# Rewriting a gather-heavy kernel: one product per batch of gathers, four key sets per search, and an order planned by the kernel itself

## The chip, the cores and the metric

The kernel runs on one core of one Trainium2 chip. The metric is device time in microseconds (us), lower is better. The names of the engines are those of the profile: PE multiplies matrices (PEld loads its weights), DVE is the vector engine, ACT the engine for activations, POOL the general one that also issues the gathers, SP the one that issues most other transfers.

## The reference

`x` is A_q, 2048 tokens of 448 numbers; `xn` is its layer norm. The output is x + A(xn) + B(xn).

```python
def A(q, k, v, shift_k, ssm_k, ssm_D):
    kv = causal_conv4(k, shift_k) * v                    # per channel, 4 taps
    y = irfft(rfft(kv, 4096) * rfft(ssm_k, 4096))[:2048]  # per channel, along the tokens
    return q * (y + kv * ssm_D)

def B(x, w_q, k1, k2, u, v):                 # 16 heads, 64 keys of 256 numbers in k1 and in k2
    q = einsum("nd,dhc->nhc", x, w_q)        # c = 512: one half for k1, one for k2
    s1, s2 = q[..., :256] @ k1.T, q[..., 256:] @ k2.T      # (2048, 16, 64) each
    # the two best of s1 and of s2 make four sums; the two best sums are two experts
    # out of 64 * 64, with softmax weights g
    act = gelu(einsum("nd,nhkd->nhk", x, u[top_e]))
    return einsum("nhk,nhk,nhkd->nd", g, act, v[top_e])
```

Each token so needs 32 rows of `u` and 32 of `v`, by computed indices: 65536 rows of 896 numbers (u and v side by side), 235 MB.

## The kernel before

The 2048 tokens are 16 tiles T of 128. For each head, `weights` multiplies w_q by the keys, so that the scores are one product of the tokens with a 448 x 2048 matrix, held in two parts (high and low) for precision. `scores(T)` transposes a tile, makes 4 groups of 512 scores in PSUM (11 matmuls each, L198 to L202), and finds in each of the 32 sets of 64 keys the 8 largest (`max`, L205) and their places (`max_index`, L206); a dozen small DVE operations choose two experts per head, and DVE transposes write the indices to `idx`.

The experts' part works in batches: a batch is 4 gathers (`gather`, L253, an indirect DMA on POOL's queue), each of 128 rows of u and v, that is 4 tokens x 32 slots. There are 8 batches k per tile, 128 in all, and a ring of 12 buffers of one gather. In `dots`, a matmul with `sel` (L266) copies each of the four token rows to its 32 partitions in PSUM, and DVE multiplies with the gathered rows and sums (L268). `values` applies gelu and gate (ACT L271, DVE L276) and multiplies with the v half of the rows into one PSUM bank `pv` (L279). `fold` adds a finished tile to `acc`.

The convolution is an FFT as matmuls: `conv_in` (taps, first stage, L335 to L362), `spectrum` (L372 to L383), `inverse` (L391 to L403), `conv_out` (L413 to L431), in two groups of 56 x 4 channels. It is cut into units with rough costs and follows the scores in one stream `work`; after every batch `fill` takes as many units as fit in the room of one batch:

```python
ROOM = (3.6, 2.9, 4.6, 0.7)
            with tc.high_priority(offset=500):
                dots(T, k)
                values(T, k)
                for o in order[4 * b + NBUF:4 * b + 4 + NBUF]:
                    gather(*o)
            fill(ROOM)
```

A scheduler of the framework orders the instructions of each engine from these priorities. PSUM has four pools of two banks.

Of the kernel before, what the change touches and what calls it, by code (L numbers as in the profile page):

```python
# [17 lines left out]
P = 128  # L18
S, D, H, E = 2048, 448, 16, 64
NT = S // P  # L20
KC = 3
KR = D - P * KC
# [9 lines left out]
GC = 56  # L32
BC = 8
KV0, H0, SK0, D0, BW = 67, 131, 195, 199, 200


def fft_tables():
# [32 lines left out]
    const = np.concatenate([f1.reshape(P, -1), ci.reshape(P, -1), tw.reshape(P, -1), f3.reshape(P, -1) / N], axis=1)  # L70
    return const.astype(np.float32), fq.reshape(NQ, P, P).astype(np.float32)


F1W, CIW, TWW, F3W = 2 * NQ * CH, 4 * P, 17 * 3, 16 * CH


@with_exitstack
def parallel_kernel(ctx, tc, x, wq, kk, uv, kvh, const, fq, out):
    nc = tc.nc
    ap = ctx.enter_context(tc.tile_pool(name="ap", bufs=1))  # L80
    rp = ctx.enter_context(tc.tile_pool(name="rp", bufs=2))
    gp = ctx.enter_context(tc.tile_pool(name="gp", bufs=NBUF))
    ps_sc = ctx.enter_context(tc.tile_pool(name="ps_sc", bufs=2, space=bass.MemoryType.PSUM))
    ps_xr = ctx.enter_context(tc.tile_pool(name="ps_xr", bufs=2, space=bass.MemoryType.PSUM))
    ps_a = ctx.enter_context(tc.tile_pool(name="ps_a", bufs=2, space=bass.MemoryType.PSUM))
    ps_v = ctx.enter_context(tc.tile_pool(name="ps_v", bufs=2, space=bass.MemoryType.PSUM))

    acc = ap.tile([P, NT, D], F32, name="acc")
    xn = ap.tile([P, NT, D], F32, name="xn")
    kks = ap.tile([P, 4, E], F32, name="kks")  # L90
    nc.scalar.dma_start(kks, kk)

    def load_x(t0, t1):
        nc.sync.dma_start(acc[:, t0:t1, :], x[t0:t1].rearrange("t p d -> p t d"))


    ident = ap.tile([P, P], F32, name="ident")
    sel = ap.tile([P, 64, 32], F32R, name="sel")
    rmask = ap.tile([P, 4], F32, name="rmask")
    cc = [ap.tile([P, 4, 32], F32, name=f"cc{k}") for k in range(8)]  # L100

    def sel_and_masks():
        make_identity(nc, ident)
        # sel[p, j, s] = 1 where p mod 64 == j
        nc.vector.tensor_add(sel, ident[:, 0:64, None].broadcast_to([P, 64, 32]),
                             ident[:, 64:128, None].broadcast_to([P, 64, 32]))
        # rmask[p, r] = 1 where p div 32 == r
        nc.vector.reduce_sum(rmask, ident.rearrange("p (r s) -> p r s", s=32), axis=mybir.AxisListType.X)
        for k in range(8):
            nc.gpsimd.memset(cc[k], 0.0)  # L110
# [6 lines left out]
    def norm(t0, t1):  # L117
        sl, n = slice(t0, t1), t1 - t0
        for t in range(t0, t1):
            st = rp.tile([P, 6], F32, tag="st", name="st")  # L120
            nc.vector.bn_stats(st, acc[:, t, :])
            nc.vector.bn_aggr(mv[:, t, :], st)
        # 1/sqrt(var + eps): a guess from the exponent, then Newton's steps to full precision
        va, y0, y1 = (rp.tile([P, NT], F32, tag=f"n{i}", name=f"n{i}")[:, :n] for i in range(3))
        nc.vector.tensor_scalar(va, mv[:, sl, 1], 1e-5, None, op0=ALU.add)
        nc.vector.tensor_scalar(y1.bitcast(I32), va.bitcast(I32), 1, None, op0=ALU.logical_shift_right)
        nc.vector.tensor_scalar(y0.bitcast(I32), y1.bitcast(I32), -1.0, float(0x5F3759DF), op0=ALU.mult, op1=ALU.add)
        for i in range(4):
            nc.vector.tensor_mul(y1, y0, y0)
            nc.vector.tensor_mul(y1, y1, va)  # L130
            nc.vector.tensor_scalar(y1, y1, -0.5, 1.5, op0=ALU.mult, op1=ALU.add)
            nc.vector.tensor_mul(y0 if i < 3 else rstd[:, sl], y1, y0)
        nc.vector.scalar_tensor_tensor(nmr[:, sl], mv[:, sl, 0], -1.0, rstd[:, sl], op0=ALU.mult, op1=ALU.mult)
        for t in range(t0, t1):
            nc.scalar.activation(xn[:, t, :], acc[:, t, :], AF.Identity, bias=nmr[:, t:t + 1], scale=rstd[:, t:t + 1])

    ws_ctx = ExitStack()
    wp = ws_ctx.enter_context(tc.tile_pool(name="wp", bufs=1))
    wh = wp.tile([P, KC, S], F32R, name="wh")
    wl = wp.tile([P, KC, S], F32R, name="wl")  # L140
    # the last 64 rows: high part above, low part below
    wr = wp.tile([P, S], F32R, name="wr")

    state = {}

    def transposes(pt, src, permute):
        for c in range(KC + 1):
            n = P if c < KC else KR
            o = pt[:n, P * c:P * c + P]
            if permute:  # L150
                o = o.rearrange("p (r c k) -> p c k r", r=4, c=4)
            nc.tensor.transpose(o, src[:, P * c:P * c + n], ident)

    def weights(h):
        ww = []
        for half in range(2):
            w = gp.tile([P, 2 * D], F32, tag="uv", name="wq")
            state["wq"] = nc.sync.dma_start(w.rearrange("p (c d) -> p c d", c=2),
                                                       wq[h, 2 * half:2 * half + 2].rearrange("c p d -> p c d"))
            ww.append(w)  # L160
        pw = ps_a.tile([P, 512], F32, tag="a", name="pw")
        for i in range(2):
            for half in range(2):
                nc.tensor.matmul(pw[64 * half:64 * half + 64, :D], kks[:, 2 * half + i, :], ww[half][:, D * i:D * i + D],  # L164
                                 start=(i == 0), stop=(i == 1), tile_position=(0, 64 * half))
        ws = wp.tile([P, D], F32, tag="ws", bufs=2, name="ws")
        nc.scalar.activation(ws, pw[:, :D], AF.Copy)
        pt = ps_xr.tile([P, 512], F32, tag="xr", name="pt")
        transposes(pt, ws, False)
        hs = slice(128 * h, 128 * h + 128)  # L170
        ptv = pt[:, :P * KC].rearrange("p (c n) -> p c n", c=KC)
        nc.scalar.activation(wh[:, :, hs], ptv, AF.Copy)
        nc.scalar.activation(wr[:KR, hs], pt[:KR, P * KC:], AF.Copy)
        nc.vector.tensor_sub(wl[:, :, hs], ptv, wh[:, :, hs].bitcast(F32))
        nc.vector.tensor_sub(wr[KR:, hs], pt[:KR, P * KC:], wr[:KR, hs].bitcast(F32))

    idx = ap.tile([P, NT, NG], I32, name="idx")
    gt = ap.tile([P, NT, NG], F32, name="gt")

    def scores(T):  # L180
# [353 lines left out]
```

## Time and profile before

| | |
|---|---|
| median of 3 runs | 1082.19 us (1070.23 to 1082.56) |
| profiled execution | span 1089.4 us |
| PE, DVE, ACT, POOL busy | 846.0, 771.3, 326.2, 551.0 us |
| bytes moved | 274.29 MB, mean 252 GB/s |
| mean granted PE clock | 0.860 |

The profile is of one execution, 7 us longer than the median; its own time is its span. A group of instructions is written as line, engine, operation, output <- input, count, then busy time and mean duration, then the idle time of the engine ahead of it and what ended most of it. In a timeline a row has start, duration, engine, line and operation. Durations on one engine can overlap by about a tenth of a microsecond, so the pitch from start to start is what counts in a full engine. Windows list the busy time of PE, PEld, DVE, ACT and POOL, and end with the granted PE clock, the DMA engines' busy share and GB/s.

### The profile page before, as it was taken

How to read it: one execution, taken by the hardware profiler on the slowest of the kernel's cores; microseconds unless marked ns; L12 is line 12 of the kernel's file. 1: busy time of each engine (PE TensorE's matmuls, PEld its weight loads, DVE VectorE, ACT ScalarE, POOL GpSimd, SP SyncE). 2: the span in 40 equal slices, each digit the busy share in tenths (PEclk: the TensorE clock that was granted, in tenths of full speed). 3: DMA queues.
4: the chain of work that ended last, by engine and by line, in shares of the span. 5: the costliest groups of instructions: out<-in, count | busy, mean ns of one | idle time of the engine just before them, and what ended most of it. 6: DMA issues, size and time to landing. Idle time of an engine off the chain costs nothing.

```text
span 1089.4 us, 15169 instructions
## 1 busy us (share of the span) xinstructions
PE 846.0 (78%) x4124; PEld 465.0 (43%) x4124; DVE 771.3 (71%) x3474; ACT 326.2 (30%) x952; POOL 551.0 (51%) x596
## 2 busy tenths in 40 slices
PE   7946778878968787777767667898987876789883
PEld 3422444434434444444433434354564443345472
DVE  4466667877789877787875545699947665599941
ACT  4313201111111110111114553366422564355421
POOL 1025255465656455455564354655558554555533
PEclk9975888888889888788986877899987888899987
DMA  9928458678778777577888776988767876888753
GB/s 340 338 95 296 152 202 270 201 273 270 267 238 263 253 252 249 200 252 259 270 274 313 257 264 204 305 284 285 254 236 268 285 256 233 292 276 268 243 200 135
DMA packets 65973, 274.29 MB, mean 252 GB/s; under 512 B 10336, under 2 KB 31200, under 8 KB 65888
## 3 DMA queue, kind: packets, MB, share of 16 engines
q0 software_dynamic: 40960, 234.91, 63.8%
q1 hardware_dynamic: 24784, 38.28, 10.1%
q8 instruction: 33, 0.54, 0.2%
q14 instruction: 52, 0.43, 0.1%
q10 hardware_dynamic: 144, 0.13, 0.0%
HBM read 269.61 MB, written 3.67 MB: 251 GB/s over the span
## 4 chain that ended last, share of the span: by engine, by line
PE 42%; DVE 32%; issue 12%; another core or an unknown queue 6%; ACT 3%; DMA 3%; POOL 1%; DVEq 0%; SPq 0%; POOLq 0%; ACTq 0%
DVE xr L268 11%; PE xr L266 8%; PE pv L279 7%; DVE mi L206 6%; PE ps L359 5%; DVE mx L205 4%; PE sc L198 3%; PE pw L164 3%; PE sc L199 3%; PE sc L200 3%; PE fin L420 3%; DVE tt L380 2%; DVE y L382 2%; ACT pr L339 2%
## 5 line engine op out<-in xcount | busy, mean ns | idle before, releaser
L253 POOL DMA_INDIRECT uv<-in_uv_dram,idx x512 | 492.2, 961 | 486.3 <-PE pv L279 139.0
L268 DVE SCALAR_TENSOR_TENSOR xr<-xr,uv 128x448 f32<-128x448 f32 x512 | 316.3, 625 | 114.0 <-remote 40.9
L266 PE MATMUL xr<-ab,sel 128*128 128x448 f32 x512 | 246.9, 518 | 144.1 <-DVE xr L268 97.2
L266 PEld LDWEIGHTS xr<-ab,sel 128*128 128x128 f32 x512 | 99.3, 210 | 293.9 <-DVE xr L268 173.4
L205 DVE MAX8 mx<-sc 128x8 f32<-128x64 f32 x512 | 110.3, 216 | 68.0 <-remote 30.0
L279 PE MATMUL pv<-uv,cc 128*32 128x448 f32 x1024 | 146.3, 648 | 8.7 <-DVE cc L276 6.6
L271 ACT ACTIVATE ge<-act 128x4 f32<-128x4 f32 x128 | 26.1, 204 | 325.6 <-DVE xr L268 210.3
L206 DVE FIND_INDEX8 mi<-mx,sc 128x8 uint32<-128x64 f32 x512 | 113.3, 222 | 0.1
L198 PE MATMUL sc<-wh,xh 128*128 128x512 f32 x192 | 89.9, 468 | 12.4 <-DVE xl L190 5.3
L199 PE MATMUL sc<-wl,xh 128*128 128x512 f32 x192 | 83.7, 436 | 0.1
L200 PE MATMUL sc<-wh,xl 128*128 128x512 f32 x192 | 82.5, 430 | 0.0
L268 DVE DVE_READ_ACCUMULATOR xr<-xr,uv 128x1 f32 x512 | 69.9, 136 | 0.6
L372 PE MATMUL psf<-x,fm 128*128 128x448 f32 x132 | 64.1, 573 | 2.1 <-issue 1.7
L362 ACT ACTIVATE x<-ps 128x396 f32<-128x396 f32 (+1 forms) x84 | 37.9, 458 | 83.8 <-PE ps L359 40.3
L198 PEld LDWEIGHTS sc<-wh,xh 128*128 128x128 f32 x192 | 42.2, 220 | 45.8 <-issue 26.8
L339 ACT ACTIVATE pr<-stg 128x64 f32<-128x64 f32 x224 | 56.0, 336 | 8.0 <-DMA stg<-in_kvh_dram 6.9
L359 PE MATMUL ps<-cst,stg 128*64 128x132 f32 x448 | 42.9, 339 | 16.1 <-DVE stg L349 9.2
L359 PE MATMUL ps<-cst,pr 128*64 128x132 f32 x448 | 40.0, 323 | 19.1 <-ACT x L362 8.4
L206 DVE MATCH_VALUE_LOAD mi<-mx,sc 128x8 f32 x512 | 42.7, 83 | 10.1 <-remote 1.7
L359 PEld LDWEIGHTS ps<-cst,stg 128*64 128x64 f32 x448 | 32.9, 170 | 35.0 <-issue 21.5
L199 PEld LDWEIGHTS sc<-wl,xh 128*128 128x128 f32 x192 | 42.3, 220 | 9.2 <-issue 0.7
L392 PE MATMUL psu<-y,cst 128*128 128x224 f32 x132 | 39.3, 380 | 8.9 <-DVE y L383 7.3
(98 smaller groups left out, 1069.3 us busy)
## 6 DMA issues: line engine op xcount, KB each, us to landing
wq<-in_wq_dram SPq DMA_DIRECT2D x32, 448.0 KB
stg<-in_kvh_dram SPq DMA_DIRECT2D x14, 800.0 KB
uv<-in_uv_dram,idx POOLq DMA_INDIRECT x512
fm<-in_fq_dram SPq DMA_DIRECT2D x66, 64.0 KB
out_dram<-acc SPq DMA_DIRECT2D x16, 224.0 KB
acc<-in_x_dram SPq DMA_DIRECT2D x2, 1344.0 KB
acc<-in_x_dram SPq DMA_DIRECT2D x1, 672.0 KB
cst<-in_const_dram SPq DMA_DIRECT2D x1, 445.5 KB
```

The costliest lines, as they stand in the source:

```text
L198: nc.tensor.matmul(sc, xh[:, c, :], wh[:, c, ns], start=(c == 0), stop=False)
L199: nc.tensor.matmul(sc, xh[:, c, :], wl[:, c, ns], start=False, stop=False)
L200: nc.tensor.matmul(sc, xl[:, c, :], wh[:, c, ns], start=False, stop=False)
L205: nc.vector.max(mx[:, 8 * n + j, :], sc[:, 64 * j:64 * j + 64])
L206: nc.vector.max_index(mi[:, 8 * n + j, :], mx[:, 8 * n + j, :], sc[:, 64 * j:64 * j + 64])
L253: nc.gpsimd.indirect_dma_start(buf, None, uv, bass.IndirectOffsetOnAxis(ap=idx[:, T, g:g + 1], axis=0))
L266: nc.tensor.matmul(xr[:, :D], sel[:, t:t + 4, :].rearrange("p a b -> p (a b)"), ab[c // 2], start=True, stop=True)
L268: nc.vector.scalar_tensor_tensor(xr[:, :D], xr[:, :D], 1.0, rows[T, k, c][:, :D], op0=ALU.mult, op1=ALU.mult, accum_out=act[:, c:c + 1])
L279: nc.tensor.matmul(pv[32 * c:32 * c + 32, :D], cc[k][:, c, :], rows.pop((T, k, c))[:, D:], start=(k == 0), stop=(k == 7), tile_position=(0 ...
L339: nc.scalar.activation(pr[t][:, c, :], stg[:, c, 3 - t:67 - t], AF.Copy, scale=stg[:, c, SK0 + t:SK0 + t + 1])
L359: nc.tensor.matmul(ps[64 * i:64 * i + 64, w * j:w * j + w], src, f1[:, i, :], start=True, stop=True, tile_position=(0, 64 * i))
L372: nc.tensor.matmul(ps[:, :2 * CH * GC], fm, x1[:, :, q, :, :].rearrange("p c t k -> p c (t k)"), start=True, stop=True)
```

## The change

The kernel is written anew around the same mathematics. By part:

- **Batches.** A gather now brings 32 tokens x 4 slots, so partition p of gather r belongs to token 32 r + p mod 32. `spread(T)` writes each quarter of a tile to all 128 partitions of one of four PSUM banks (`xs`) with a 32-row matmul, once per tile and not once per gather. One DVE multiplication of 4 x 448 takes a whole batch; ACT sums each of the four products; gelu on ACT; two POOL multiplications make the coefficients; four matmuls with blocks of 32 columns add up in one bank. The ring has 5 batches (20 buffers). A gather waits for the landing of the sixth before it.
- **Searches.** The two largest of 8 key sets stand side by side, and one `max_index` looks up the 8 values of four sets in their 256 scores. An index outside its own set is noted (`lo`, `hi`). After the pass a flag is loaded, and if it is set, a whole second pass (`safe`) runs with a search for every set.
- **Indices.** They come out of masks (ACT) and a matmul (`place`) instead of DVE transposes, for the first tile a quarter of the heads at a time.
- **Convolution.** Two parts, 28 and 84 of the 112 groups of 4 channels; the first runs beside the scores, the second after them. The four taps are one DVE multiplication; the tap additions are on POOL in the first part and on DVE in the second.
- **Output.** `fold` reloads `x`, adds `pv` and stores the tile. The convolution's part of tiles 0 to 13 is added in DRAM by 14 accumulating transfers, which stand at the end of POOL's queue; tiles 14 and 15 add it before their store.
- **Order.** A list planner (`Plan`) in the kernel sorts all operations by due times and assumed durations while the program is built; the framework keeps that order on each engine. PSUM holds `xs` (4 banks), `pv` (1) and 3 banks that all else shares.

The core of the diff:

```diff
-NG = 32
-NBUF = 12
-ROOM = (3.6, 2.9, 4.6, 0.7)
+NB = 8
+RING = 5
+PARTS = ((0, 28), (28, 84))
+T_OUT0, T_OUT1 = 9, 14
...
+class Plan:
+    def op(self, eng, dur, fn, r=(), w=(), key=0.0, acq=None, rel=None, nb=0.0, name="", after=()):
...
+T0, PACE, PACE2 = 51.5, 5.4, 4.5
+TURN = 58
+OUTSTANDING = 6
+LIGHT = 200
...
+    xs = pp.tile([P, 4, 512], F32, name="xs")
+    pv = pp.tile([P, 512], F32, name="pv")
+    bank = [pp.tile([P, 512], F32, name=f"bank{i}") for i in range(3)]
...
-            for j in range(8):
-                nc.vector.max(mx[:, 8 * n + j, :], sc[:, 64 * j:64 * j + 64])
-                nc.vector.max_index(mi[:, 8 * n + j, :], mx[:, 8 * n + j, :], sc[:, 64 * j:64 * j + 64])
+            for j in range(8):
+                nc.vector.max(mx[:, 8 * n + j, :] if safe else m2[:, n, 2 * j:2 * j + 8], bank[s.i][:, 64 * j:64 * j + 64])
+        def find(g):
+            if safe:
...
+            else:
+                nc.vector.max_index(m4i[:, 2 * n + g, :], m2[:, n, 8 * g:8 * g + 8], bank[s.i][:, 256 * g:256 * g + 256])
...
+                nc.vector.tensor_sub(loc[:, gs_], m4i[:, gs_], off8[:, None, :].broadcast_to([P, 2 * (b1 - b0), 8]))
+                nc.vector.tensor_tensor(lo[:, gs_], lo[:, gs_], loc[:, gs_], op=ALU.min)
+                nc.vector.tensor_max(hi[:, gs_], hi[:, gs_], loc[:, gs_])
...
-        nc.vector.transpose(idx[:, T, :], es.rearrange("p h t -> p (h t)"))
+            for q in range(4):
+                src = Ev.rearrange("p r k (j s) -> p s r k j", s=4)[:, q]
+                nc.tensor.matmul(o[32 * q:32 * q + 32, :8 * nj], rep, src, start=True, stop=True, tile_position=(0, 32 * q))
...
-            nc.tensor.matmul(xr[:, :D], sel[:, t:t + 4, :].rearrange("p a b -> p (a b)"), ab[c // 2],
-                             start=True, stop=True)
-            nc.vector.scalar_tensor_tensor(xr[:, :D], xr[:, :D], 1.0, rows[T, k, c][:, :D], op0=ALU.mult, op1=ALU.mult,
-                                           accum_out=act[:, c:c + 1])
+    def spread(T):
+            for r in range(4):
+                rs = slice(32 * r, 32 * r + 32)
+                nc.tensor.matmul(xs[:, r, :D], i4[rs, :], XA[rs, T, :], start=True, stop=True, tile_position=(32 * r, 0))
+    def batch(T, j):
...
+        op("DVE", dve(m * D), lambda: nc.vector.tensor_mul(U[:, :m, :], U[:, :m, :], xs[:, :m, :D]), r=["xs"], w=u[:m], key=k, name="prod")
...
+        for r in range(m):
+            op("ACT", 0.72, lambda r=r: nc.scalar.activation(U[:, r, :], U[:, r, :], AF.Copy, accum_out=aw[:, r:r + 1]),
...
+        def coef():
+            ve.tensor_mul(co, ge, gat[:, T % 8, :, j])
+            ve.tensor_mul(cc[b % 3], co[:, :, None].broadcast_to([P, 4, 32]), rep[:, None, :].broadcast_to([P, 4, 32]))
+        def val():
+            for r in range(4):
+                nc.tensor.matmul(pv[32 * r:32 * r + 32, :D], cc[b % 3][:, r, :], ring[:, b % RING, r, D:],
+                                 start=(j == 0), stop=(j == NB - 1), tile_position=(0, 32 * r))
...
+    for T in range(0, T_OUT1):
+        i = op("POOL", 1.0, lambda T=T: nc.gpsimd.dma_start(out[T], XA[:, T, :], accum_op=ALU.add), r=[("x", T)], key=CONV["out1"][1], after=(stored[T],), name="accum")
...
+    order = pl.solve()
+    with tc.manual_schedule():
+        for o in order:
+            o.fn()
...
+def parallel_kernel(tc, *args):
+    with tc.tile_pool(name="flag", bufs=1) as pool:
+        flag = pool.tile([1, 1], I32, name="flag")
+        one_pass(tc, *args, flag)
+        found = tc.nc.values_load(flag, min_val=0, max_val=P * 64)
+        with tc.If(found > 0):
+            one_pass(tc, *args, None)
```

With 128 batches and LIGHT = 200, `m` is 4 and `ve` is POOL in every batch.

More of the change, by code (lines that the diff above doesn't have):

```diff
@@ L100, in parallel_kernel @@
[L100 to L110, printed above, removed]
+    pp = ctx.enter_context(tc.tile_pool(name="pp", bufs=1, space=bass.MemoryType.PSUM))
@@ L115, in parallel_kernel @@
     nmr = ap.tile([P, NT], F32, name="nmr")
[L117 to L135, printed above, removed]
@@ L154, in weights @@
-    def weights(h):
[L155 to L175, printed above, removed]
```

975 lines of the change are left out of this document (654 added, 321 removed).

## The prediction

> **What bounds the kernel now.** I read the page first: span, busy shares and the chain that ended last.
>
> ```profile
> span 1089.4 us, 15169 instructions
> PE 846.0 (78%) x4124; PEld 465.0 (43%) x4124; DVE 771.3 (71%) x3474; ACT 326.2 (30%) x952; POOL 551.0 (51%) x596
> DMA packets 65973, 274.29 MB, mean 252 GB/s; under 512 B 10336, under 2 KB 31200, under 8 KB 65888
> PE 42%; DVE 32%; issue 12%; another core or an unknown queue 6%; ACT 3%; DMA 3%; POOL 1%; DVEq 0%; SPq 0%; POOLq 0%; ACTq 0%
> DVE xr L268 11%; PE xr L266 8%; PE pv L279 7%; DVE mi L206 6%; PE ps L359 5%; DVE mx L205 4%; PE sc L198 3%; PE pw L164 3%; PE sc L199 3%; PE sc L200 3%; PE fin L420 3%; DVE tt L380 2%; DVE y L382 2%; ACT pr L339 2%
> ```
>
> No engine is full. The chain is a relay between PE and DVE: PE spreads the token rows over 128 partitions (L266), DVE multiplies and sums them with a gathered row (L268), PE spreads the next. The groups and the view of waits say the same of both ends.
>
> ```profile
> L253 POOL DMA_INDIRECT uv<-in_uv_dram,idx x512 | 492.2, 961 | 486.3 <-PE pv L279 139.0
> L268 DVE SCALAR_TENSOR_TENSOR xr<-xr,uv 128x448 f32<-128x448 f32 x512 | 316.3, 625 | 114.0 <-remote 40.9
> L266 PE MATMUL xr<-ab,sel 128*128 128x448 f32 x512 | 246.9, 518 | 144.1 <-DVE xr L268 97.2
> PEld xr L266 <- DVE xr L268: 173.4, 146, 5.8
> POOL uv L253 <- PE pv L279: 139.0, 53, 12.4
> ```
>
> The spread waits for DVE; the gathers wait for PE to release a row buffer. One batch (4 gathers, 128 rows each) costs 1089.4 / 128 = 8.5 us. The profiled span is 1089.4 us against a median of 1082.2; I make the sum in the profiled time and leave the 7 us difference alone.
>
> **The change, part by part.** All 512 gathers stay. I price each engine for one batch, or for a block of 8 batches (one tile of tokens), then see which engine is longest.
>
> *POOL.* The timeline of POOL shows the pitch of its instructions, which is not their duration:
>
> ```profile
> 226.15 0.95 POOL L253 DMA_INDIRECT uv<-in_uv_dram,idx  x1 [0.31 <-issue]
> 227.12 1.16 POOL L241 TENSOR_TENSOR hi<-xn,hi 128x448 fp32r<-128x448 f32 x1
> 228.44 0.96 POOL L253 DMA_INDIRECT uv<-in_uv_dram,idx  x1 [0.16 <-issue]
> 229.70 0.95 POOL L253 DMA_INDIRECT uv<-in_uv_dram,idx  x1 [0.30 <-DVE pair L218]
> L431 POOL TENSOR_TENSOR acc<-acc,yg 128x160 f32<-128x160 f32 x7 | 3.7, 525 | 5.7 <-DVE yg L429 5.7
> L431 POOL TENSOR_TENSOR acc<-acc,yg 128x32 f32<-128x32 f32 x7 | 1.8, 254 | 19.0 <-DVE yg L429 19.0
> ```
>
> Gather to gather takes 229.70 - 228.44 = 1.26 us though a gather is busy 0.95; the 0.30 recurs with "issue" as its cause, so I count 1.25 us each. With an op of 1.16 between, gather to gather is 2.29: the op costs its duration less 0.12. The change puts two POOL multiplies (4 and 128 elements) into every batch. From 254 ns at 32 and 525 at 160 elements, the 128-element one is about 0.46 and the small one at most 0.25, near 0.19: together 0.65 less 0.12 and a 0.05 overlap, 0.48. A batch costs POOL 4 x 1.25 + 0.48 = 5.5 us, a block 44; all 128 batches 704. POOL loses the `hi` and `acc` adds and gets 14 tap adds (13 us in all) and, behind the last multiply, 14 accumulating stores.
>
> *DVE.* Its timeline gives the pitches:
>
> ```profile
> 216.46 0.21 DVE L205 MAX8 mx<-sc 128x8 f32<-128x64 f32 x1
> 216.59 0.61 DVE L268 SCALAR_TENSOR_TENSOR xr<-xr,uv 128x448 f32<-128x448 f32 x1
> 217.12 0.14 DVE L268 DVE_READ_ACCUMULATOR xr<-xr,uv 128x1 f32 x1
> 217.12 0.08 DVE L206 MATCH_VALUE_LOAD mi<-mx,sc 128x8 f32 x1
> 217.19 0.22 DVE L206 FIND_INDEX8 mi<-mx,sc 128x8 uint32<-128x64 f32 x1
> 217.33 0.61 DVE L268 SCALAR_TENSOR_TENSOR xr<-xr,uv 128x448 f32<-128x448 f32 x1
> ```
>
> A 448-element product takes 0.53 from start to start, a maximum 0.13, a search 0.07 + 0.14. Removed: 512 product-sums. Added: 128 products of 1792 elements, at most 4 x 0.53 = 2.1 us; without three start-ups of 0.06, 1.94. A search over 256 elements costs 192 elements more at the 0.47 / 448 that the product pays per element, 0.41 instead of 0.21, but there are 128 and not 512. So a group of 8 key sets costs 8 x 0.13 + 2 x 0.41 = 1.86 us instead of 2.7. While the scores last, a block holds on average 8 products (15.5), 8 groups (14.9), two choices of experts with their range checks (3.4), the low half of the tokens, the fold and a share of the convolution (8): 42 us, under POOL's 44.
>
> *PE.* The 512 spreads by `sel` go; each tile gets four 32-row matmuls into the four banks of `xs` instead, 16 x 4 in all: 0.2 to 1 us each by the rows here, taken as 1.3 us a tile.
>
> ```profile
> 216.54 0.42 PE L198 MATMUL sc<-wh,xh 128*128 128x512 f32 x1
> 218.95 0.50 PE L202 MATMUL sc<-wr,xl 64*128 64x512 f32 x1
> 219.38 0.68 PE L266 MATMUL xr<-ab,sel 128*128 128x448 f32 x2
> 219.98 0.96 PE L279 MATMUL pv<-uv,cc 128*32 128x448 f32 x8
> 220.87 0.47 PE L266 MATMUL xr<-ab,sel 128*128 128x448 f32 x1
> ```
>
> A score group of 11 takes 219.38 - 216.54 = 2.84 us, a batch of values 0.89. A block in the first half: 8 x 2.84 + 8 x 0.89 + 1.3 + transposes and convolution 7 = 38 us at full clock. At the mean clock of before it is 44, the length of POOL's block:
>
> ```profile
> core 0: 1089.4 us, clock 0.860
> ```
>
> *ACT.* New: 512 activations that sum a product along 448 elements. Not seen here; the nearest are a plain copy and a scaled one of the same size.
>
> ```profile
> L240 ACT ACTIVATE hi<-xn 128x448 fp32r<-128x448 f32 x16 | 9.1, 570 | 14.2 <-POOL acc L291 12.1 <-issue 2.0
> L135 ACT ACTIVATE xn<-acc,nmr,rstd 128x448 f32<-128x448 f32 x16 | 10.8, 751 | 0.5 <-DVE nmr L133 0.5
> L375 ACT ACTIVATE hh<-psf 128x224 f32<-128x224 f32 x66 | 23.5, 356 | 31.0 <-PE psf L372 17.4 <-issue 8.9 <-DVE xr L268 2.0
> ```
>
> Bounds: 0.47 (0.57 less the 0.10 by which ACT's instructions overlap) and 0.75 + 0.14, DVE's price for reading a sum. I take 0.67, nearer the plain copy. A block is 32 x 0.67 + 8 x 0.23 = 23 us, plus 10 to 14 for scores and convolution. In the fullest block (batches 96 to 104: 15 spectra of three 0.46 us copies, 14 twiddles) it reaches 50, 6 over POOL. At 0.89 each it would be 57 there and about POOL's length elsewhere: 20 us more in all.
>
> *DMA.* The 274.3 MB grow by 16 re-reads of `x` (3.7) and the accumulating stores (6.4): 284 MB. What the engines can carry, from windows of the trace (last three columns: clock, DMA share, GB/s):
>
> ```profile
> 0.00:27.00 27.00, 21.21 (x79) 8.17 (x80) 11.30 (x36) 11.46 (x26) 2.98 (x15) 1.00 0.96 340
> 27.00:54.00 27.00, 27.00 (x122) 11.90 (x121) 13.59 (x64) 9.34 (x24) 0.00 (x0) 1.00 0.96 341
> 578.00:588.00 10.00, 4.68 (x33) 2.73 (x32) 2.73 (x7) 4.84 (x18) 7.46 (x8) 0.50 1.02 414
> 606.00:616.00 10.00, 3.27 (x40) 2.41 (x34) 2.84 (x8) 3.95 (x15) 5.84 (x7) 0.89 1.01 403
> ```
>
> At 403 to 414, a 0.459 MB gather takes 1.11 to 1.14 us, below POOL's 1.37 (5.5 / 4). So gathers with a fifth of extra traffic just fit. The Trainium skill speaks against this: "DMA: Bandwidth & Descriptors", section "Where 436 GB/s comes from", says that between HBM and SBUF the HBM side binds at about 358 GB/s. By it 284 MB would take an estimated 793 us, 828 with the tail below; the 414 above, over 10 us, does not agree with it, and no window here shows whether it holds for hundreds of us.
>
> *The start.* Weights, tokens and constants are 19 MB. Each quarter of the heads now yields its indices alone, so gathers start near 30 us, but share the DMA: 19 MB and 24 gathers (11 MB) at 340 GB/s are 88 us. The last quarter's chain (scores 2.84, search 1.9, choice, masks, placing) adds about 8 and its 8 gathers 10: batch 8 starts gathering at about 105 us. Before, gathers began just ahead of the one at 72.85 quoted below, with the loads done.
>
> *The tail.* After the last gather: landing, product 1.94, four sums 2.7, gelu and multiply 0.9, then 14 accumulating stores that POOL holds behind that multiply, 14 x 1.25 = 17.5 and a landing.
>
> ```profile
> 72.85 5.09 DMA uv<-in_uv_dram,idx
> ```
>
> 5 + 1.9 + 2.7 + 0.9 + 17.5 + 3 = 31 us, and 5 for loading the flag and the branch (not seen here; 2 to 10).
>
> *Sum.* 105 + 480 gathers x 1.37 (658) + tap adds 13 + 31 + 5 = 812 us if POOL never waits. But in the first half PE, DVE and POOL are all at 38 to 44 of 44 us, in a fixed order, with three PSUM banks for everything. Some waiting must come. The bound from above is the share of the old chain in which nothing ran, issue 12% and unknown 6%: 18% of 671 is 120 us. With rows in 20 buffers instead of 12, I take 4%, 28 us: **840 us**. Ends: 812 and 932.
>
> **Rivals.**
>
> *Gathers without the pause.* If the 0.30 us belongs to the old waits of L253 and not to a gather, DMA is the bound: 284 MB at 403 is 705, plus the tail 36: **742 us**. For: gather to `hi` is only 0.97. Against: 0.30 stands in every pair, whatever released it.
>
> *Memory holds at 340.* 284 / 0.340 = 835 + 36 = **871 us**. For: two windows of 27 us in a row stay there. Against: those are 1792-byte rows; the gathers' windows pass 400. (The page of the Trainium skill named above has the same mechanism, at 358.)
>
> *The order costs more.* If the fullest engine only reaches 80%, as DVE did in the old stage where scores and gathers ran together,
>
> ```profile
> 200.00:300.00 100.00, 83.99 (x333) 45.28 (x333) 77.82 (x487) 13.12 (x39) 57.15 (x61) 0.86 0.76 257
> ```
>
> a block is 44 / 0.8 = 55 us: 105 + 15 x 55 + 36 = **966 us**. For: every engine now waits in a written order, behind a late landing too. Against: POOL's stream depends on results five batches back.
>
> *The second pass runs.* Slower. The search over four key sets returns the first match, so a value that an earlier set of the four also holds gives an index out of 0 to 63; one such value in the whole input sets the flag, and after the last store all is done again with single searches. Price: 840 again plus 64 x 1.0 us of DVE time, partly hidden: **1700 us**. It decides from one equal pair on. From the reference's inputs in double precision, 339 pairs of a set's two best and another set's scores lie within 1e-4; float32 steps at these values are 1e-7 to 5e-7, so 0.2 equal pairs are expected, 0.11 to 0.13 of them with the earlier set. Against: most likely none.
>
> **How the numbers follow.** Forecast 0.50 (812 to 900), no pause 0.14, memory 0.10, order 0.13, second pass 0.13. The likeliest is the forecast, 840 us. From 740 to 945 lie the forecast, the memory case, two thirds of the fast one and a third of the order: eight in ten. Slower by over 2% (about what a measurement here tells from no change) is the second pass, 0.13; the order case at its worst reaches no change, 0.01; faster 0.86.
>
> **What would show it.** Right: POOL shows 1.25 us from gather to gather and few waits for PE; the product is one DVE op near 2.0 us x128; ACT sums near 0.7 x512; PE busy falls by about 150 us; the 14 stores end the chain. Wrong: gathers waiting mainly for their sixth predecessor's landing (DMA binds), for PE (the order binds), pitches of 0.97, or a program whose every instruction count is doubled.

## The result, and the profile after

The changed kernel takes 1029.14 us (median of 4, 1026.43 to 1037.06) against 1082.38 us for the kernel before (1070.23 to 1091.31, 4 runs beside it): ratio 0.9546, 95% interval 0.9479 to 0.9613. It is faster, but the 840 us forecast was far off, and the range (740 to 945) does not hold the result. The second pass did not run. The profiled execution has a span of 1029.6 us; its page:

```profile
span 1029.6 us, 14196 instructions
PE 699.9 (68%) x3976; PEld 410.0 (40%) x3976; DVE 710.8 (69%) x1780; ACT 533.4 (52%) x1783; POOL 618.5 (60%) x802
DMA packets 72216, 281.34 MB, mean 273 GB/s; under 512 B 10816, under 2 KB 35648, under 8 KB 72128
DVE 24%; PE 23%; issue 18%; POOL 14%; DMA 9%; another core or an unknown queue 5%; ACT 4%; DVEq 0%; POOLq 0%; SPq 0%; ACTq 0%
L513 POOL DMA_INDIRECT ring<-in_uv_dram,idx x512 | 504.3, 985 | 253.2 <-issue 114.5
L551 ACT ACTIVATE ring<-ring 128x448 f32<-128x448 f32 x512 | 288.4, 567 | 83.6 <-DVE ring L545 70.5
L551 ACT ACTIVATION_READ_ACCUMULATOR ring<-ring 128x1 f32 x512 | 97.4, 190 | 0.0
L545 DVE TENSOR_TENSOR ring<-ring,xs 128x1792 f32<-128x1792 f32 x128 | 257.1, 2016 | 92.8 <-DMA ring<-in_uv_dram,idx 71.4
L427 DVE FIND_INDEX8 SC<-SC,bank 128x8 uint32<-128x256 f32 x128 | 52.6, 423 | 0.0
L556 POOL TENSOR_TENSOR sm<-sm,gat 128x4 f32<-128x4 f32 x128 | 30.9, 241 | 117.9 <-ACT sm L553 114.3
L557 POOL TENSOR_TENSOR cc<-sm,c 128x128 f32<-128x128 f32 x128 | 56.5, 442 | 15.4 <-PE pv L562 5.4
```

Most operations cost what was forecast: one product of 2.0 us a batch (1.94 foretold), a search over 256 elements 423 ns (0.41), a sum 0.47 + 0.09 = 0.56 from start to start (0.67, within its bounds). Two do not, the maxima and the pair of coefficients (below). PE fell by 146 us of busy time (150 foretold). What is not as forecast: POOL, meant to be the full engine, is busy for 60% of the span, 75% with the 0.30 us after each of the 512 gathers. Now POOL's timeline:

```profile
114.00 0.97 POOL L513 DMA_INDIRECT ring<-in_uv_dram,idx  x1 [0.30 <-issue]
115.28 0.95 POOL L513 DMA_INDIRECT ring<-in_uv_dram,idx  x1 [0.30 <-issue]
116.54 0.94 POOL L513 DMA_INDIRECT ring<-in_uv_dram,idx  x1 [0.30 <-issue]
117.79 0.95 POOL L513 DMA_INDIRECT ring<-in_uv_dram,idx  x1 [0.30 <-issue]
123.56 0.26 POOL L556 TENSOR_TENSOR sm<-sm,gat 128x4 f32<-128x4 f32 x1 [4.82 <-ACT sm L553]
```

The pitch of 1.25 us with its 0.30 pause is there. Then POOL stands 4.82 us at the multiply that waits for the gelu of an older batch, and the next gathers stand behind it. The view of waits, whole run (engine, line, awaited; us in total, times, longest):

```profile
POOL sm L556 <- ACT sm L553: 114.3, 33, 8.8
PEld pv L562 <- POOL cc L557: 73.8, 39, 6.9
DVE ring L545 <- DMA ring<-in_uv_dram,idx: 71.4, 26, 9.1
ACT ring L551 <- DVE ring L545: 70.5, 27, 7.7
POOL ring L513 <- PE pv L562: 49.4, 40, 6.5
ACT idx L498 <- remote: 28.1, 6, 12.6
DVE S L604 <- remote: 17.7, 5, 7.2
```

Everybody waits a little for everybody: gathers for values, values for coefficients, coefficients for sums, sums for products, products for landings. From the start of each gather and the end of each batch's values in the timeline: batch 8's first gather starts at 130.3 us, the last of the 480 gathers from there at 988.2 (1.79 us a gather, not 1.37), and 41 us follow. The values of the first block end at 137.9, those of the sixteenth at 1000.6, 57.5 us a block.

### The profile page after: what moved, and what is told of

Same layout as the page of the kernel before. It is cut to its first block, busy times and chain, and to the rows that moved or that the text cites. A ratio compares the mean times of both kernels' runs of the same rounds, so it can differ in the third digit from the quotient of the medians.

```text
span 1029.6 us, 14196 instructions
## 1 busy us (share of the span) xinstructions
PE 699.9 (68%) x3976; PEld 410.0 (40%) x3976; DVE 710.8 (69%) x1780; ACT 533.4 (52%) x1783; POOL 618.5 (60%) x802
## 4 chain that ended last, share of the span: by engine, by line
DVE 24%; PE 23%; issue 18%; POOL 14%; DMA 9%; another core or an unknown queue 5%; ACT 4%; DVEq 0%; POOLq 0%; SPq 0%; ACTq 0%
POOL ring L513 10%; DVE SC L420 7%; DMA ring<-in_uv_dram,idx 6%; DVE ring L545 6%; PE pv L562 5%; PE bank L621 4%; DVE SC L427 3%; PE bank L747 2%; DMA R<-in_wq_dram 2%; ACT ring L551 2%; POOL cc L557 2%; PE bank L699 2%; DVE S L678 1%; PE bank L700 1%
## 5 line engine op out<-in xcount | busy, mean ns | idle before, releaser
L513 POOL DMA_INDIRECT ring<-in_uv_dram,idx x512 | 504.3, 985 | 253.2 <-issue 114.5
L551 ACT ACTIVATE ring<-ring 128x448 f32<-128x448 f32 x512 | 288.4, 567 | 83.6 <-DVE ring L545 70.5
L545 DVE TENSOR_TENSOR ring<-ring,xs 128x1792 f32<-128x1792 f32 x128 | 257.1, 2016 | 92.8 <-DMA ring<-in_uv_dram,idx 71.4
L562 PE MATMUL pv<-ring,cc 128*32 128x448 f32 x1024 | 148.5, 664 | 97.3 <-POOL cc L557 57.3
L420 DVE MAX8 SC<-bank 128x8 f32<-128x64 f32 x512 | 118.4, 231 | 28.9 <-PE bank L415 6.3
L621 PE MATMUL bank<-c,S 128*64 128x132 f32 x896 | 84.8, 349 | 34.7 <-ACT ring L551 14.9
L411 PE MATMUL bank<-WR,xh 128*128 128x512 f32 x192 | 88.9, 463 | 13.3 <-issue 6.1
L621 PEld LDWEIGHTS bank<-c,S 128*64 128x64 f32 x896 | 69.5, 178 | 70.6 <-ACT ring L551 27.8
L551 ACT ACTIVATION_READ_ACCUMULATOR ring<-ring 128x1 f32 x512 | 97.4, 190 | 0.0
L412 PE MATMUL bank<-WR,xh 128*128 128x512 f32 x192 | 83.7, 436 | 0.3 <-DVE WR L371 0.3
L413 PE MATMUL bank<-WR,xl 128*128 128x512 f32 x192 | 82.5, 430 | 0.8 <-DVE xl L401 0.8
L678 DVE TENSOR_TENSOR S<-bank,S 128x224 f32<-128x224 f32 (+1 forms) x66 | 40.9, 619 | 13.9 <-remote 9.2
```

The lines of the kernel that those rows point to most:

```text
L411: nc.tensor.matmul(o, xh[:, c, :], wh[:, c, ns], start=(c == 0), stop=False)
L412: nc.tensor.matmul(o, xh[:, c, :], wl[:, c, ns], start=False, stop=False)
L413: nc.tensor.matmul(o, xl[:, c, :], wh[:, c, ns], start=False, stop=False)
L420: nc.vector.max(mx[:, 8 * n + j, :] if safe else m2[:, n, 2 * j:2 * j + 8], bank[s.i][:, 64 * j:64 * j + 64])
L513: g = nc.gpsimd.indirect_dma_start(dst, None, uv, bass.IndirectOffsetOnAxis(ap=idx[:, T % 8, r, j:j + 1], axis=0)).ins
L545: op("DVE", dve(m * D), lambda: nc.vector.tensor_mul(U[:, :m, :], U[:, :m, :], xs[:, :m, :D]), r=["xs"], w=u[:m], key=k, name="prod")
```

## The experiments

In the short diffs "-" is the changed kernel and "+" the experiment; blocks are timed as just said. Ratios are to the kernel before on the same chip; the changed kernel was not run again beside them. Experiments 1 to 4 ran on four chips on which the kernel before took 1087 to 1095 us (medians), experiment 5 on another, on which it took 956; more on this there.

**1. Is it the loop through gelu and coefficients?** POOL waits most for gelu. Three runs: the coefficients to DVE; the planner told the measured gather pitch, landing and coefficient time; the dot products left out.

```
coef_dve     - ve = nc.vector if light else nc.gpsimd
             + ve = nc.vector
plan_times   - HOP DMA 1.6, gather 0.97, coef 0.2 + pool_t(128)
             + HOP DMA 2.7, gather 1.25, coef 0.85
no_dots      - prod, sum, gelu, coef (L545 to L558); values use a constant cc
```

> The two small multiplications that make a batch's coefficients go from POOL to DVE (256 instructions; the planner orders anew, with 0.46 us on DVE for 0.66 us on POOL). Theory 1, POOL's queue: gathers stand behind a multiplication that waits 114 us for gelu, and 49 us for values; without it POOL's stream is gathers alone, and the time falls by 50 to 110 us, to 920 to 980, with POOL's waits for ACT gone. Theory 2, the ring and the written order on DVE and PE: DVE gains 128 x 0.3 us of work and a wait of its own, so 1010 to 1070. Theory 3, DMA or memory rate: no change, 1020 to 1040.

> Only numbers that the planner assumes change: a gather takes POOL 1.25 us and not 0.97, its landing 2.7 us after the transfer and not 1.6, a coefficient pair 0.85 us and not 0.66; so the order of instructions changes, and nothing else. If the order was written for gathers that land 1.3 us too early (engines then stand at a product whose rows are late), time falls by 30 to 100 us, to 930 to 1000, and DVE's 71 us of waiting for landings shrinks. If the ring of five batches or the engines' own work bounds it, 1015 to 1045.

> Leaves out the products, sums, gelu and coefficients of all batches: the values are multiplied with constant coefficients as soon as the rows land. Gathers, scores, convolution and stores stay. If the gathers' pitch of 1.25 us on POOL or the memory's rate were the bound, the time stays within 5% of 1030 (rate held at 340 GB/s: 870). If the loop landing - product - sums - gelu - coefficients - values that holds a row buffer is what costs, the time falls to 760 to 860, near the 812 that POOL's pitch alone gives.

coef_dve: 1058.92 us, ratio 0.9742 (0.9613 to 0.9870): no faster than the changed kernel's 0.9546, and rather slower, with intervals that touch. plan_times: 1017.97 us, 0.9376 (0.9264 to 0.9489), its interval touching the changed kernel's from the other side. Its gathers are no quicker: in the profiles, batch 8 starts gathering at 121.0 us instead of 130.3, the 480 gathers from there take 887 us instead of 858, and 19 us instead of 41 follow. no_dots: 1052.15 us, 0.9697 (0.9527 to 0.9868), although 257 us of DVE and 386 of ACT fell away. Its first-half blocks last 66 to 76 us. By its expectation this points at the gathers' pitch or the memory; no_conv and gather_thin below speak against both. POOL's largest wait looks like a symptom: in no_dots, with its cause removed, another has taken its place:

```profile
POOL ring L513 <- PE pv L547: 219.1, 49, 15.7
```

But no_dots's trace also holds 469 us of waits that the view can put down to nothing (rows "<- remote", experiment 4), against 127 in the changed kernel. So it does not show what the loop costs where those are absent.

**2. Which other stream holds it?** Without the convolution; the same with a ring of 7 batches; without the scores of 15 tiles, whose gathers use tile 0's indices.

```
no_conv        - conv_first, conv_mid, conv_last, gated
no_conv_ring7  - RING = 5
               + RING = 7, wqb: 2 buffers instead of 4       (and no_conv)
one_score      - scores(T) for T > 0, idx[:, T % 8], gat[:, T % 8]
               + idx[:, 0], gat[:, 0]
```

> Leaves out the whole convolution (the output lacks its part); batches, scores, gathers and stores stay, ring of 5. If DVE, PE and ACT work that stands in the written order between a batch's steps is the cause, the second half, which then holds batches alone, runs at POOL's 5.7 us a batch and the time falls to 800 to 880, while the first half, still with scores, stays above 6.5 us a batch. If the loop of a batch by itself is longer than five batches' time, the second half stays at 6.5 to 7 us a batch and the time above 930.

> As no_conv (the whole convolution is left out; 910 us), but a ring of 7 batches instead of 5, in the room that the convolution leaves. If the time that a row buffer is held (26 us from a batch's last gather to the end of its values, over five batches) sets the pace, the first half falls from 53 us a block of 8 batches towards POOL's 46 and the time to 850 to 875. If the engines' waits for each other in the written order set it, whatever is buffered, 895 to 915.

> Leaves out the scores of tiles 1 to 15: all tiles gather by tile 0's indices (512 gathers of the same size), batches, convolution and stores stay. If the scores' work on PE and DVE between a batch's steps costs the first half its time, blocks there fall from 62 us to 46 to 50 and the time to 850 to 910. If the convolution's steps are as much to blame, blocks stay above 55 and the time above 950.

no_conv 910.09 us, ratio 0.8388 (0.8233 to 0.8543); no_conv_ring7 918.64, 0.8484 (0.8375 to 0.8594); one_score 910.72, 0.8411 (0.8305 to 0.8517). With either stream gone the time is 910, with both there 1029. no_conv lies between the ranges of its two theories: its second half runs at POOL's pace (below), its first half at 56 us a block. The seven batches of no_conv_ring7 shorten the stretch from batch 8's first gather to the last from 765 to 745 us, and the first half's blocks only from 56 to 55; but batch 8 starts 24 us later (152 instead of 127), where two buffers for w_q instead of four made room for the ring. So without the convolution a longer ring would bring a little, and with it none was tried. Windows of no_conv, where from 600 us on only batches are left (busy time of PE, PEld, DVE, ACT, POOL; clock, DMA share, GB/s):

```profile
600.00:700.00 100.00, 32.10 (x152) 4.40 (x152) 36.67 (x20) 43.36 (x153) 76.31 (x104) 0.52 0.94 325
700.00:800.00 100.00, 33.03 (x160) 4.62 (x160) 34.53 (x19) 43.37 (x153) 77.61 (x106) 0.52 0.95 315
```

A block there takes 46 us, 5.8 a batch: four gathers at 1.25 and a coefficient pair at 0.7. This is POOL's floor, seen undisturbed, and the transfers carry it.

**3. Is the order mistimed, or one shared resource too small?** More of the planner's durations as I read them off the trace (plan_all), due times stretched too (plan_all_due); seven PSUM banks instead of three, in no_dots; the turned tile kept twice (xh2, and with plan_times); indices of 16 tiles instead of 8.

```
plan_all        + as plan_times; PE x 1.2, search 0.15 and 0.41, sum 0.56
plan_all_due    + as plan_all; PACE 6.3 and 5.8, SC_END 450, CONV later
no_dots_7banks  - bank ... for i in range(3), xs, spread(T)
                + bank ... for i in range(7)     (and no_dots)
xh2             + xhs[T % 2], xls[T % 2]; Eb in zt
idx16           - idx, gat: 8 tiles
                + 16 tiles
xh2_times       + xh2 and plan_times
```

> All durations that the planner assumes are set to what this kernel's trace shows: gather 1.25, coefficient pair 0.85, landing 1.1 later, PE's groups 1.2 times longer (its granted clock is 0.8), sums 0.56, maxima 0.15 each, search 0.41, product 1.94. Due times stay. Instructions are the same, the order is new. If mistimed orders make the engines wait for each other, 940 to 1000 (plan_times, with POOL's part alone, took 1018). If not, 1010 to 1040.

> As plan_all, and the due times of batches, scores and convolution are stretched to a pace of 6.3 and 5.8 us a batch (scores done by 450, convolution 205 to 735). If the mistimed order is the cause, this is the best of the orders: 900 to 980. If the first half is bound by chains of scores and convolution through three PSUM banks, 1000 to 1050.

> As no_dots (products, sums, gelu and coefficients left out, the values taken with constant coefficients; 1052 us, 66 to 72 us a block in the first half), and the spread of x (line 531) left out too, which frees four PSUM banks: scores and convolution share seven banks instead of three. Theory 'three banks': a step of scores or convolution mostly waits for a free bank, so with seven the first half goes to 46-50 us a block and the whole to 870-930. Rival 'single buffers along the chain' (xh and xl, the stages of the convolution, the eight tiles' indices): banks don't matter, the first half stays at 62-70 us a block and the whole at 1000-1060.

> The whole changed kernel with xh and xl (the turned tile that the score matmuls read) kept twice, so the turn of the next tile needn't wait for the last score matmul of this one (the masked indices Eb move to zt to make room). Theory 'score chain': some 5 to 8 us of each tile's turn come beside the scores of the tile before, 7 blocks of the first half get 5-8 us shorter: 960-1000. Rival 'three banks' or 'PE in order': the turn fits in elsewhere already, 1015-1045.

> The whole changed kernel with indices and weights of sixteen tiles kept instead of eight, so the search of tile T+8 needn't wait until tile T's last gather and coefficients are through (the trace has ACT waiting 28 us at the write of idx, 6 times, with the search behind it). Theory 'index buffers couple search and batches': 980-1005, the largest gaps of the first half (70, 79, 74 us a block) go. Rival 'three banks' or 'PE in order': 1015-1045.

> xh and xl kept twice, and the order planned with the measured gather pitch, landing and coefficient time (plan_times: 1018). If the score chain's turn sets the first half, the two add up: 945-990. If not, as plan_times, 1005-1030.

plan_all 1054.34 us, 0.9765 (0.9655 to 0.9875); plan_all_due 1062.41, 0.9803 (0.9708 to 0.9899); no_dots_7banks 1049.40, 0.9660 (0.9585 to 0.9735); xh2 1038.43, 0.9534 (0.9462 to 0.9606); idx16 1037.14, 0.9558 (0.9496 to 0.9620); xh2_times 1027.49, 0.9453 (0.9386 to 0.9520). None of the single resources tried here sets the time, and none of these runs is set apart from the changed kernel as faster; plan_all and plan_all_due are slower. Two limits: no_dots_7banks carries 426 us of rows "<- remote", as no_dots does, and seven banks were not tried with the products in place. And plan_all's 0.15 for a maximum is not what the trace shows from one maximum to the next, 0.27 (below; the changed kernel's plan has 0.216), so the two plans do not show what an order with true durations would take.

**4. Why do TensorE's results come late?** The trace of the changed kernel holds a wait that the program does not explain. PE's timeline, then ACT's, in the same stretch:

```profile
388.32 0.42 PE L493 MATMUL bank<-SC,c 128*32 128x64 f32 x8 [0.99 <-DVE S L683]
390.15 0.39 PE L700 MATMUL bank<-S,c 128*128 128x112 f32 x2
401.17 1.11 PE L665 MATMUL bank<-R,S 128*128 128x224 f32 x2 [10.64 <-ACT gat L500]
```

```profile
387.70 0.57 ACT L484 ACTIVATE SC<-SC,c 128x64 f32<-128x64 f32 x2
400.84 0.20 ACT L498 ACTIVATE idx<-bank 128x32 int32<-128x32 f32 x1 [12.57 <-remote]
```

L498 waits for the placing matmuls of L493. These end at 388.74, PE's last record ends at 390.54, and ACT gets its signal at 400.84; PE itself then waits for ACT. No index buffer holds it either: in idx16, which has one for every tile, L498 still has 23.6 us of such rows. "remote" is what the view writes when it finds no instruction that ended a wait; on a program with one core there is no other core. Rows "<- remote" sum to 127 us in the changed kernel and to 159 in the kernel before, of which the prediction quoted 40.9 at L268 without asking what they were. Four runs asked whether transfers or value matmuls cause it:

```
gather_thin  - dst = ring[:, b % RING, r, :], uv
             + 16 of the 896 numbers of a row; the ring is filled once
val_thin     - pv[..., :D], ring[..., D:]
             + 16 columns
out4, out8   - OUTSTANDING = 6
             + 4, 8
```

> The whole changed kernel, but each gather brings 16 numbers a row instead of 896 (a 56th of the bytes, from the first rows of the table); the rest of the ring is filled once with a constant on POOL at the start. The same 512 gather instructions, products, sums, values, scores and convolution, so the same instructions and semaphores on every engine. Theory 'transfers hold TensorE back' (in the changed kernel the trace has consumers of TensorE results waiting some 107 us in all after its last record has ended, in steps of 0.7 and 1.4 us, while gathers run): these waits nearly vanish and the time falls to 850-940, POOL's own sum being about 870. Rival 'the order and the serial steps of the engines alone': the waits stay and the time falls by little, to 970-1030.

> The whole changed kernel, but the value matmuls take 16 columns instead of 448 (the rest of the result bank is zeroed once): the same instructions, order, semaphores and transfers, with some 0.9 us of streaming less in each of 128 batches. Theory 'value matmuls cost TensorE far more than their records show' (four tiles of 32 columns each, streamed one after the other, 3 to 6 us a batch): the late results vanish and the time falls to 860-940. Theory 'transfers hold TensorE back': the late results stay, the time falls by at most the 0.9 us x 128 that stand in the records, of which TensorE was waiting for half: 960-1020. Rival 'the order alone': the same 960-1030, with the late results as before.

> The changed kernel with at most four gathers on their way instead of six. Theory 'transfers hold TensorE back': fewer packets queued, fewer late results: 1000-1025. Rival 'TensorE's lateness has nothing to do with how much is queued': POOL loses some cover and the time is the same or slower, 1025-1070.

> The changed kernel with at most eight gathers on their way instead of six. Theory 'transfers hold TensorE back': more packets queued, more late results: 1030-1060. Rival 'what is queued doesn't matter': the same within 1% (1020-1040).

gather_thin: 1044.23 us (1035.98 to 1052.48, two runs too far apart for a ratio); with a 56th of the gathered bytes (17 to 59 GB/s in the windows from 100 to 800 us) it is no faster, and its remote rows sum to 212 us. val_thin: 1030.02 us, 0.9408 (0.9302 to 0.9513), remote 144. out4: 1031.20, 0.9410 (0.9318 to 0.9503), remote 35. out8: 1044.14, 0.9555 (0.9467 to 0.9644), remote 148. So neither the bytes nor the value columns set the time, nor do they make results late. out4 has a quarter of the remote rows at the same time: their sum can't simply be taken off the total.

**5. What of the scores holds the rest?** Three matmuls a set instead of eleven; or all work kept, but every gather with tile 0's indices.

```
score_short  - 11 matmuls (L411 to L415)
             + 3 (first 128 of 448 numbers)
free_index   - idx[:, T % 8], gat[:, T % 8]
             + idx[:, 0], gat[:, 0] for gathers and coefficients
```

> The changed kernel with 3 matmuls a set instead of 11 in the scores (the first 128 of 448 numbers and one correction term), so the search finds other, valid slots; every step, wait, search and gather stays. 64 x 8 matmuls of 0.23 us fall away from TensorE, 118 us at full clock. Theory 'TensorE is what fills up, by its own streaming': the late results and the time shrink, 900-950. Rival 'the fixed order and the serial steps between engines, whose number stays': the time barely moves, 990-1030.

> The changed kernel with the scores and the search of all tiles done as before, but every tile's gathers and coefficients take tile 0's indices and weights, so that no gather waits for a search and no search for a gather; TensorE, VectorE and ScalarE do the same work in nearly the same order. Theory 'gathers wait for the search that runs late': as one_score, 905-940. Rival 'scores and convolution hold the values, on TensorE, by work and steps': 1000-1035.

These two ran on the other chip. There the kernel before took 956.17 us (951.29 to 960.01, 15 runs), score_short 956.95 (ratio 1.0009, 0.9976 to 1.0041) and free_index 956.93 (1.0005, 0.9979 to 1.0031). Neither trace has a single "<- remote" row. The first rows of free_index's view of waits:

```profile
PEld pv L562 <- POOL cc L557: 148.4, 72, 7.2
PE pv L562 <- POOL cc L557: 119.7, 54, 6.9
ACT ring L551 <- DVE ring L545: 106.4, 60, 7.9
POOL sm L556 <- ACT sm L553: 50.2, 18, 6.4
ACT idx L498 <- PE bank L493: 8.6, 4, 6.3
```

The row of L498, "remote" before, now names the matmul it waits for. Windows of the first half, the changed kernel (first chip) and then free_index (other chip):

```profile
250.00:350.00 100.00, 74.29 (x354) 46.59 (x353) 78.30 (x277) 41.54 (x156) 52.49 (x69) 0.84 0.67 232
350.00:450.00 100.00, 67.56 (x340) 43.04 (x339) 73.12 (x228) 48.56 (x181) 56.06 (x75) 0.80 0.70 243
sum 400.00, PE 276.30 PEld 174.45 DVE 300.69 ACT 191.83 POOL 236.23; mean PE 69.08 PEld 43.61 DVE 75.17 ACT 47.96 POOL 59.06
```

```profile
250.00:350.00 100.00, 75.04 (x383) 47.77 (x382) 88.59 (x280) 57.45 (x215) 64.55 (x89) 0.88 0.83 291
350.00:450.00 100.00, 73.58 (x396) 47.32 (x395) 87.96 (x302) 52.32 (x194) 64.02 (x84) 0.89 0.83 287
sum 400.00, PE 310.03 PEld 196.57 DVE 343.66 ACT 220.89 POOL 269.15; mean PE 77.51 PEld 49.14 DVE 85.91 ACT 55.22 POOL 67.29
```

On the other chip DVE is the fullest engine, 86% from 150 to 550 us; a block takes 52.4 us over the run and 53.4 in that part (values of the second block end at 198.8, of the ninth at 573). Taking PE's matmuls away (score_short) or the tie between search and gathers (free_index) ends at the same 957; DVE's work is left whole by both, and no run on this chip took any of it away. The expectations were written for the first chip, so their figures can't be held against these times, only the pattern: two different cuts, one time. The changed kernel itself was not run on the other chip; whether it beats the kernel before there is open. These two, which have less to do or less to wait for, only equal it.

## Why the prediction was wrong

The sum was made of the start, 480 gathers at 1.37 us, tap adds, waiting, tail. Beside the profile (1029.6):

| term | predicted | measured |
|---|---|---|
| to batch 8's first gather | 105 | 130.3 |
| 480 gathers, tap adds and waiting | 658 + 13 + 28 | 858 |
| after the last gather | 36 | 41.4 |

**The step that failed** is "I take 4%, 28 us" of waiting, on top of "42 us, under POOL's 44" for DVE. At POOL's prices the 480 gathers and tap adds are 671 us, and 28 more for the under-sized coefficient pair (below); they took 858, so 159 us of waiting, 23%. I had a bound on this (18% of the old chain, 120 us, itself too low) and chose far below it because "rows in 20 buffers instead of 12" should cover it.

**DVE's block was under-sized**, by the maxima. Eight of them, and the search behind them, in DVE's timeline; then the window of the second to the eighth block:

```profile
119.63 2.10 DVE L420 MAX8 SC<-bank 128x8 f32<-128x64 f32 x8
121.65 0.07 DVE L427 MATCH_VALUE_LOAD SC<-SC,bank 128x8 f32 x1
137.90:586.30 448.40, 311.07 (x1659) 196.76 (x1655) 334.67 (x1063) 209.36 (x766) 267.33 (x353) 0.82 0.74 254
```

The eight take 2.02 us, 0.27 from one to the next. I took 0.13 from a row of before in which a product follows the maximum. Now each maximum follows another, writes its 8 values two places further on, over six of that one's, and starts only 0.03 us after that one has ended. (That the shared places are the reason is argued from the program; no run gave them places of their own.) A group is 2.02 + 2 x 0.4 = 2.8 us and not 1.86, eight groups 22.5 and not 14.9, DVE's block 49.6 and not 42. The window agrees: 334.67 / 7 = 47.8 us busy, and some 2 us of these gaps. So while the scores last DVE is the longest engine, not POOL (45.9 with the right price of the pair), and by this estimate some 26 us of the 159 (seven blocks, 3.7 us each) are no loss of overlap but work that was priced too low.

**Where the rest of the waiting came from**, as far as shown: batches, scores and convolution together, in one written order, and none of the single resources tried. With only two of the three streams half of it goes (no_conv, about 79 us left) or two thirds (one_score, 52, which also has almost no maxima left), and a block of batches alone is 46 us, within 2 of the forecast. Of the three engines that I put at 38 to 44 us of a 44 us block, PE and DVE serve all three streams and POOL two, each in order; that an operation late on one holds the others' next ones is argued from this. Experiments 1 and 3 fit: lift a single wait and the time stays.

**The rival "The order costs more"** named the mechanism and also fell short, by its 80% (the row it quotes has PE at 84 and DVE at 78). With DVE's measured 75% its formula gives 105 + 15 x 44 / 0.75 + 36 = 1021, near the 1029.6; but this is a sum made afterwards, and it puts DVE's share on POOL's 44 in all 15 blocks, so the nearness is in part luck. Its chance of 0.13 was too low: three engines within 15% of each other, three streams and a fixed order make it the likely case. The cases counted into the range add up to 0.74, too, and not to eight in ten. Of the signs for being wrong none fits: POOL waits most for gelu, and its gathers 49 us for PE and 4 for landings.

**The start** was 25 us short, by two things. The last quarter's indices came 12 us late (108.4; the sum has 88 + 8). Its 8 gathers took the 10 us foretold. But batch 8 is the first of tile 1, and the sum has no term for tile 1's own search. POOL, PE and ACT in turn:

```profile
108.40 0.97 POOL L513 DMA_INDIRECT ring<-in_uv_dram,idx  x1 [2.00 <-ACT gat L500]
94.54 0.96 PE L562 MATMUL pv<-ring,cc 128*32 128x448 f32 x8 [2.29 <-issue]
129.86 0.20 ACT L498 ACTIVATE idx<-bank 128x32 int32<-128x32 f32 x1 [0.51 <-PE bank L493]
130.33 0.97 POOL L513 DMA_INDIRECT ring<-in_uv_dram,idx  x1 [1.44 <-ACT gat L500]
```

Batch 8 takes the row buffers of batch 3, whose values (second row) end at 95.5: the ring does not hold it. After the last quarter's gathers POOL waits for a gelu and for the tap additions' input, and is released by ACT's write of tile 1's indices and weights. In free_index, where no gather waits for a later tile's search, batch 8 starts at 118.6, though on the other chip.

**Right:** the gather's pitch; the product, search and sum; PE's fall; the tail, within 5 us. In the tail the 5 us for the flag and the branch rested on no row: POOL's load of the flag takes 1.48 us and ends at 1018.6, 0.6 after the last store is issued, and 11 us follow until the span ends. The pair of coefficients was under-sized: in a run of gathers that wait for nothing, the one at 89.58 and the next, at 91.54, stand 1.96 apart with a pair between them, so 0.71 for the pair against 0.48, because nothing overlaps where I took 0.17 off. That is 29 us over 128 batches.

**The other rivals.** "Gathers without the pause" fell by the pitch; "The second pass" did not run. "Memory holds at 340" is not what bounds the kernel, since gather_thin is no faster without the bytes; and its ceiling was passed. The fullest window of 100 us found in these runs, in plan_all, moved 367 GB/s:

```profile
630.00:730.00 100.00, 65.17 (x639) 41.97 (x637) 75.83 (x96) 61.69 (x206) 76.96 (x95) 0.81 0.98 367
```

The Trainium skill, "DMA: Bandwidth & Descriptors", section "Where 436 GB/s comes from", puts the HBM side's limit at about 358 GB/s. This window passes it, so the trace does not agree.

**What stays open.** What 0.13 us a maximum would bring was not run. And results of PE reach their consumers up to 12.6 us late on the first chips and, in the two runs on the other one, never. It is not the gathers' bytes and not the values' columns. They came late before the change (159 us of rows) as after (127). What share of the 1029 it is, can't be said: the two runs without it differ from the changed kernel in a part of the program as well as in the chip. If free_index's cut tie is worth nothing, it is the 72 us between the two, and the other 117 us above the forecast stay on a chip without late results. In score_short and free_index the 840 us is missed by these 117, with DVE at 86% in the first half.

## What to carry to other kernels

When several engines are within 15% of each other and serve several streams in one fixed order, don't price the result by the fullest engine plus a few per cent: price it by the share that the fullest engine reached in the old stage where the same streams ran together, and take a lower one if there are now more of them in order. Read an instruction's cost from a row in which the same neighbours follow as in the new program: a pitch of 0.13 became 0.27 when each maximum had to wait for the one before. A first look at the rows "<- remote" of a one-core trace is cheap: they are waits that the program can't explain, and their sum went from 35 to 469 us between edits of this kernel, so look at it before a run is read as a test of something else. An engine's largest wait is a symptom until a run without its cause is faster.

## What the runs showed of the hardware

The kernel before took 1082 to 1095 us on some chips and 956 on another, 12% apart. The traces on the first have waits for PE of up to 12.6 us that the view can put down to no instruction, those on the other have none. The granted clock of the kernel before is 0.85 to 0.87 on the first and 0.90 to 0.93 on the other; whether it makes the difference or follows from it was not tried. The first chips' traces also lack events: PE's semaphore (the counter that tells other engines of its results) has 799 recorded updates for the 965 matmuls that raise it in the changed kernel, 982 for 981 in free_index; whether the gaps and the delays have one cause was not tried. Eight maxima in a row whose outputs overlap stand 0.27 us apart; in the kernel before, 0.13 us after a maximum the next instruction starts. A gather instruction has the same 1.25 us pitch whether it brings 3584 bytes a row or 64.
